# Linear attention into a soft mixture of experts: one DVE reduction moved ahead of another, a maximum taken a tile later, and input loads regrouped

## The chip, the cores and the metric

One core of a Trainium2 chip runs the kernel. The metric is device time in microseconds (us) of one execution, as the median of several runs; lower is better. Before the change it is 174.96 us (median of 3 runs, 174.92 to 174.98). All data is float32. Engines are named as in the profile: PE (matrix products), PEld (its weight loads), DVE, ACT and POOL (element by element work), SP (issues the transfers). Every transfer of this kernel is issued by SP on one queue, which 16 DMA engines serve.

## The reference

Eight batches of 576 tokens with eight heads of 64 go through linear attention; each head's output row is scaled by its root mean square; the 4608 rows of 512 then go through a soft mixture of eight experts with four slots each.

```python
kv = np.einsum('bhsd,bhse->bhde', k, v)
out = np.einsum('bhsd,bhde->bhse', q, kv)
rms = np.sqrt(np.mean(out * out, axis=-1, keepdims=True) + 1e-06)
x = (out / rms * g_norm)                      # rows: (batch, token), 512 columns
logits = x @ phi                              # 4608 x 32 slots
d = softmax of logits over the 4608 tokens
slot_input = d.T @ x                          # 32 x 512, four rows per expert
slot_out[e] = np.maximum(slot_input[e] @ w1[e], 0.0) @ w2[e]
c = softmax of logits over the 32 slots
result = c @ slot_out
```

## The kernel before

**Tiles.** The 4608 tokens are 36 tiles T of 128. For each tile PE multiplies q with a block diagonal tile `bd` of k times v of the batch (`products`, L273; L264 where a tile spans two batches) and gets in one go the attention output and its share of the logits per head, 192 columns for each pair of heads, in a PSUM tile `o` with two buffers. Two tiles make a stage s (the last two stages have one tile each). Of each tile ACT takes the squares (`square`, L283), the parts of the logits (`evict`, L290) and the rows x (L291). Of each stage DVE sums the squares (`mean_square`, L296, "ms"); ACT makes a reciprocal root from that (`root`, L304 and L305); DVE refines it (`newton`, L312 to L314, "r"); POOL scales the logits' parts (`scale_part`, L345) and then the rows (`scale_x`, L323); DVE adds the parts of the eight heads up to logits (`logits`, L358).

**Groups.** Six tiles make a group G. When its last logits are there, DVE takes a maximum over the group and all before it (`group_max`, L371 and L379), PE turns it (`group_max_T`, L386), DVE reduces it (`group_max_row`, L394), ACT and PE spread it (`group_diag`, L398; `group_exp_PE`, L403), DVE and ACT make exponentials (`group_exp`, L409, L410), and PE adds up exponentials times rows (`group_sum`, L422), which DVE gathers (L429). The dictionaries `T_at`, `diag_at`, `pb_at`, `d_at` and `sums_at` say at which tile each of these steps is emitted.

**Order.** Nothing is scheduled by a tool: each engine runs its instructions in the order in which the loop over T (L487) writes them. In one turn of it stand, for DVE, `logits` of the stage that ended two tiles ago, the group's maximum, `newton` of the stage that ended one tile ago, the group's reduced row, and `mean_square` of the stage that ends now. The products of k and v of the coming batch (`kv_step`, L205 to L250) are put between the tiles. Tiles 34 and 35 and the last group are written out behind the loop (L531 to L574).

**Experts.** `expert_h(e)` (L637) multiplies the slots with w1 of expert e; `expert_y(e, hf)` (L655) multiplies the result with w2 and adds all experts up, first the left half of the columns (hf = 0), then the right half (hf = 1). `output` (L688) multiplies with the combine weights; ACT and DVE copy the result (L696, L698) and SP sends it out in six transfers (L702). Matrices w2 of experts 2 to 7 are packed by halves: units 2, 3 and 4 hold the left halves of experts 2 and 3, 4 and 5, 6 and 7, and units 5, 6 and 7 the right halves. The left halves are multiplied in the order of the experts, so unit 3 is read before unit 4.

**Loads.** Nearly all of a core's fast memory is one tile `arena` of 128 partitions, in which q, k, v, weights and results follow each other in the same places. `KV_AT`, `Q_AT`, `W_AT` and `OUT_AT` give the places (in kilobytes of a partition), `W_ROWS` says which weights come in one transfer, one row of it for each of the 128 partitions. SP issues them in the order of the program (`load_head`, L90; `load_row`, L93; `load_w`, L122), each when what stood in its place has been read: `loads_behind` ties them to tiles, the rest stand behind the loop and between the experts. "t2" is batch 4's k and v with two batches of q, "kv5" is batch 5's k and v, "t3" batches 6 and 7 with their q.

Of the kernel before, what the change touches and what calls it, by code (L numbers as in the profile page):

```python
# [14 lines left out]
P = 128  # L15
# [15 lines left out]
TOK = 4608  # L31
# [4 lines left out]
KV_AT = (0, 36, 54, 0, 90, 126, 18, 54)  # L36
Q_AT = (18, 72, 108, 36)
W_AT = {
# [3 lines left out]
}  # L42
W_ROWS = (
    (("w1", 0, None), ("w2", 0, None)),
    (("w1", 1, None), ("w2", 1, None)),
    (("w1", 2, None), ("w1", 3, None)),
    (("w1", 4, None), ("w2", 2, 1)),
    (("w1", 5, None),),
    (("w1", 6, None),),
    (("w1", 7, None),),  # L50
    (("w2", 2, 0),),
    (("w2", 3, None),),
    (("w2", 4, None),),
    (("w2", 5, None),),
    (("w2", 6, None),),
    (("w2", 7, None),),
# [1 line left out]
OUT_AT = (16, 22, 28, 34, 40, 46, 72, 128, 134, 78, 84, 90)  # L58
OUT_ROWS = ((0, 1), (2, 3), (4, 5), (6,), (7, 8), (9, 10, 11))
HEAD = 144  # L60
SCRATCH = 1024
EPS_RMS = 1e-6
EPS_SUM = 1e-9
# [4 lines left out]


@with_exitstack  # L70
def soft_moe_linear_attention(ctx: ExitStack, tc: tile.TileContext, first_in, head_in, t2_in, kv5_in, t3_in, w_in, out):


    nc = tc.nc
# [17 lines left out]
    def load_row(at, src):  # L92
        nc.sync.dma_start(place(at, src.shape[-1]), src)  # L93
# [20 lines left out]
    def load_w(kind, u, part=None):  # L114
        i = [row[0] for row in W_ROWS].index((kind, u, part))
        lo = sum(row_length(row) for row in W_ROWS[:i])
        n = row_length(W_ROWS[i])
        src = w_in[:, lo * P : (lo + n) * P].rearrange("o (p n) -> (o p) n", p=P)
        t = homes(kind, u)[part or 0]
        if n > t.shape[-1]:  # L120
            t = place(W_AT[kind, u][part or 0], n)
        nc.sync.dma_start(t, src)  # L122

    def w_block(kind, u, i):
# [16 lines left out]
    loads_behind = {  # L141
        9: lambda: load_row(KV_AT[6], t3_in),
        18: lambda: load_w("w1", 0),
        21: lambda: load_w("w1", 1),
        26: lambda: load_w("w1", 2),
        27: lambda: load_w("w1", 4),
        31: lambda: load_w("w1", 5),
    }

    nc.scalar.preload_act_table_set("natural_log_exp_and_others")  # L150
# [134 lines left out]
    def evict(T, o):  # L285
        s = stage_of[T]
        if T == starts[s]:
            parts[s] = wk.tile([P, STAGES[s], H, NS], F32, tag="part", name=f"part{s}", bufs=3)
        part = parts[s][:, T - starts[s]].rearrange("p (j w) n -> p j w n", w=2)
        nc.scalar.copy(part, o[:, :, :192].rearrange("p j (c n) -> p j c n", n=NS)[:, :, 0::5])  # L290
        nc.scalar.copy(xts[T % NX][:, :, :128], o[:, :, 32:160])  # L291


    def mean_square(s):
        mss[s] = wk.tile([P, STAGES[s] * H], F32, tag="ms", name=f"ms{s}", bufs=3)
        nc.vector.tensor_reduce(  # L296
            out=mss[s], in_=sqs.pop(s).rearrange("p t j (w d) -> p (t j w) d", w=2), axis=AX.X, op=ALU.add
        )
# [84 lines left out]
    def group_max_T(G):  # L383
        pm = ps.tile([P, P], F32, tag="m", name=f"pm{G}")
        if G in tops:
            nc.tensor.matmul(pm, lhsT=tops.pop(G).rearrange("p a n -> p (a n)"), rhs=ident, start=True, stop=True)  # L386
        for j in range(4 if G == len(GROUPS) - 1 else 0):
            nc.tensor.matmul(
                pm[32 * j : 32 * j + 32], lhsT=L[:, pos(g0[G]) + GROUPS[G]], rhs=ident, start=True, stop=True
            )  # L390
        pms[G] = pm

    def group_max_row(G):
        nc.vector.tensor_reduce(out=run_max[G % 2], in_=pms.pop(G), axis=AX.X, op=ALU.max)  # L394
# [39 lines left out]
    first = {b: 9 * (b // 2) + 4 * (b % 2) for b in range(B)}  # L434
# [48 lines left out]
    load_head(4, 2048, TOK)  # L483
    load_row(KV_AT[4], t2_in)
    load_row(KV_AT[5], kv5_in)
    T_at, diag_at, pb_at, d_at, sums_at = {}, {}, {}, {}, {}
    for T in range(NT - 2):  # L487
        for b in range(1, B):
            for at in kv_steps.get((b, T - first[b]), ()):
                kv_step(b, at)  # L490
        o = products(T)
        s = ends.get(T - 1)
        if s is not None:
            root(s)
        if T in diag_at:
            group_diag(diag_at[T])
        square(T, o)
        G = d_at.get(T)
        if G is not None:
            group_exp(G)  # L500
            sums_at[T + 1] = G
        evict(T, o)
        old = ends.get(T - 2)
        if old is not None:
            logits(old)
            if (n := group_done(old)) is not None:
                group_max(n)
                T_at[T + 1] = n
        if T in T_at:
            group_max_T(T_at[T])  # L510
            diag_at[T + 1] = pb_at[T + 2] = T_at[T]
        if s is not None:
            newton(s)
        if T in T_at:
            group_max_row(T_at[T])
        if s is not None:
            scale_part(s, nc.gpsimd)
            scale_x(s)
        if T in pb_at:
            group_exp_PE(pb_at[T])  # L520
            d_at[T + 1] = pb_at[T]
        if T in ends:
            mean_square(ends[T])
        if T in sums_at:
            todo_sums += [(sums_at[T], i) for i in range(GROUPS[sums_at[T]])]
        for _ in range(min(2, len(todo_sums))):
            group_sum(*todo_sums.pop(0))
        if T in loads_behind:
            loads_behind[T]()
# [2 lines left out]
    tail_ps = ps.tile([P, 2, 512], F32, tag="kv", name="tail")  # L532
    A, Z = NT - 2, NT - 1
    oA = products(A)
    group_exp_PE(G - 1)
    root(s - 2)
    square(A, oA)
# [18 lines left out]
    group_max(G)  # L556
    for i in todo_sums:
        group_sum(*i)
    load_w("w1", 6)
    load_w("w1", 7)  # L560
    load_w("w2", 2, 0)
    fill(LATE_FILL[0], home=ps.tile([P, 512], F32, tag="m", name="fill"), cols=512)
    group_max_T(G)
    group_max_row(G)
# [139 lines left out]
                )  # L704

    expert_h(0)
    load_w("w2", 3)
    expert_h(1)
    load_w("w2", 4)
    expert_y(0, 0)  # L710
    combine(0)
    expert_h(2)
# [36 lines left out]
def build_program():  # L749
    import concourse.bacc as bacc  # L750

    nc = bacc.Bacc("TRN2", target_bir_lowering=False, num_devices=1, dynamic_dma_scratch_size=SCRATCH)
    shapes = {
        "first": (P, HEAD + 2304), "head": (6, P, TOK), "t2": (P, 2 * TOK), "kv5": (P, TOK), "t3": (P, 3 * TOK),
        "w": (1, 2 * NE * P * UNIT),
    }
    args = [nc.dram_tensor(f"in_{n}_dram", s, F32, kind="ExternalInput").ap() for n, s in shapes.items()]
    args.append(nc.dram_tensor("out_0_dram", (1, 4 * NCH * P * 4 * CT * NS), F32, kind="ExternalOutput").ap())
    with tile.TileContext(nc, schedule_with_timeline_sim=True) as tc, tc.manual_schedule():
        soft_moe_linear_attention(tc, *args)  # L760
    return nc
# [56 lines left out]
```

## Time and profile before

| What | Value |
|---|---|
| median of 3 runs | 174.96 us |
| the profiled execution | 174.76 us, of which its span (first to last instruction) is 173.0 us |
| outside the span | 1.76 us |
| PE busy | 150.3 us (87%) |
| DVE, ACT, POOL busy | 89.1 us, 86.4 us, 57.2 us |
| moved by DMA | 71.67 MB, 414 GB/s over the span |
| read from and written to HBM by the program | 61.94 MB and 9.44 MB |

The page gives an engine's busy time, its share of the span and its instructions; 40 equal slices of the span with the busy share in tenths; the DMA queues with packets, megabytes and the time of their packets as a share of 16 engines' span; the chain of work that ended last; and groups of instructions with busy time, the mean of one in nanoseconds, and the idle time of the engine just before them with what ended most of it. A view of DMA packets in a window counts the packets that start in it, by queue and size. In this program a row of a transfer is one packet, and each DMA engine closes a transfer with one packet of 4 bytes: the page counts 512 packets under 512 B, and 32 issues on 16 engines make 512. Queues that the page calls "instruction" bring in the program's own instructions.

### The profile page before, as it was taken

How to read it: one execution, taken by the hardware profiler on the slowest of the kernel's cores; microseconds unless marked ns; L12 is line 12 of the kernel's file. 1: busy time of each engine (PE TensorE's matmuls, PEld its weight loads, DVE VectorE, ACT ScalarE, POOL GpSimd, SP SyncE). 2: the span in 40 equal slices, each digit the busy share in tenths (PEclk: the TensorE clock that was granted, in tenths of full speed). 3: DMA queues.
4: the chain of work that ended last, by engine and by line, in shares of the span. 5: the costliest groups of instructions: out<-in, count | busy, mean ns of one | idle time of the engine just before them, and what ended most of it. 6: DMA issues, size and time to landing. Idle time of an engine off the chain costs nothing.

```text
span 173.0 us, 4659 instructions
## 1 busy us (share of the span) xinstructions
PE 150.3 (87%) x1973; PEld 108.3 (63%) x1973; DVE 89.1 (51%) x184; ACT 86.4 (50%) x224; POOL 57.2 (33%) x68
## 2 busy tenths in 40 slices
PE   7788999999979899999999796989999899978500
PEld 2467978888769788888897583346666435433200
DVE  1111456566576656566664776842888433456600
ACT  2024586976947976878859465112222131315500
POOL 6000067636557753477563676600000000000000
PEclk9999999999999999999999999999999999999955
DMA  5999999999999998999999999999999999999994
GB/s 199 420 429 427 447 404 447 399 506 409 405 413 473 479 435 359 417 436 415 440 440 415 426 411 421 424 432 415 434 419 424 424 424 425 393 404 418 418 452 196
DMA packets 4628, 71.67 MB, mean 414 GB/s; under 512 B 512, under 2 KB 512, under 8 KB 640
## 3 DMA queue, kind: packets, MB, share of 16 engines
q1 hardware_dynamic: 4608, 71.38, 97.3%
q8 instruction: 15, 0.25, 0.6%
q14 instruction: 5, 0.04, 0.1%
HBM read 61.94 MB, written 9.44 MB: 413 GB/s over the span
## 4 chain that ended last, share of the span: by engine, by line
PE 54%; DVE 16%; ACT 12%; POOL 5%; issue 4%; DMA 3%; POOLq 1%; DVEq 0%; ACTq 0%
PE o L273 13%; PE pY L655 9%; PE ph L637 8%; PE kvp_kv L205 7%; PE po L688 6%; POOL part L345 4%; DVE logits L358 4%; DVE ms L296 4%; DMA arena<-in_first_dram 3%; PE pS L422 2%; ACT sq L283 2%; DVE arena L698 2%; ACT bd L240 2%; ACT xall L291 1%; ACT r L304 1%
## 5 line engine op out<-in xcount | busy, mean ns | idle before, releaser
L273 PE MATMUL o<-bd,arena 128*128 128x192 f32 x256 | 49.3, 336 | 1.6 <-ACT xall L291 0.6
L273 PEld LDWEIGHTS o<-bd,arena 128*128 128x128 f32 x256 | 41.0, 191 | 4.4 <-ACT xall L291 1.7
L345 POOL TENSOR_TENSOR part<-part,r 128x512 f32<-128x512 f32 x17 | 17.8, 1047 | 52.6 <-DVE r L314 52.6
L323 POOL TENSOR_TENSOR xall<-xall,r 128x512 f32<-128x512 f32 x34 | 34.7, 1043 | 0.0
L358 DVE TENSOR_REDUCE logits<-part 128x64 f32<-128x512 f32 (+1 forms) x18 | 18.3, 1014 | 16.5 <-POOL part L345 16.4
L296 DVE TENSOR_REDUCE ms<-sq 128x16 f32<-128x1024 f32 (+1 forms) x19 | 21.9, 1154 | 5.8 <-ACT sq L283 5.7
L283 ACT ACTIVATE sq<-o 128x512 f32<-128x512 f32 x36 | 21.4, 596 | 6.1 <-PE o L273 5.8
L291 ACT COPY xall<-o 128x512 f32<-128x512 f32 x34 | 20.7, 609 | 0.0
L205 PE MATMUL kvp_kv<-arena 128*64 128x64 f32 x480 | 17.9, 231 | 0.9 <-DMA arena<-in_first_dram 0.9
L205 PEld LDWEIGHTS kvp_kv<-arena 128*64 128x64 f32 x480 | 15.9, 144 | 4.3 <-issue 1.9
L696 ACT COPY arena<-po 128x768 f32<-128x768 f32 x12 | 9.3, 800 | 18.5 <-PE po L688 18.4
L698 DVE COPY arena<-po 128x768 f32<-128x768 f32 x12 | 11.3, 956 | 10.6 <-PE po L688 9.8
L655 PE MATMUL pY<-arena,xall 128*32 128x256 f32 x256 | 15.6, 382 | 0.5 <-DVE y L671 0.5
L688 PE MATMUL po<-logits,z 32*128 32x384 f32 x96 | 13.5, 525 | 2.1 <-DVE z L677 0.9
L637 PE MATMUL ph<-arena,sTe 128*32 128x256 f32 x224 | 12.7, 380 | 0.3 <-DVE sTe L584 0.3
L655 PEld LDWEIGHTS pY<-arena,xall 128*32 128x32 f32 x256 | 7.8, 110 | 7.8 <-issue 1.4
L290 ACT COPY part<-o 128x256 f32<-128x256 f32 x34 | 12.6, 372 | 0.0
L304 ACT ACTIVATE r<-ms,eps 128x16 f32<-128x16 f32 x17 | 5.2, 308 | 14.7 <-DVE ms L296 14.5
L422 PE MATMUL pS<-xall,d 128*32 128x129 f32 x288 | 10.8, 278 | 2.0 <-ACT d L410 2.0
L688 PEld LDWEIGHTS po<-logits,z 32*128 32x128 f32 x96 | 5.8, 183 | 8.9 <-ACT arena L696 5.0
L637 PEld LDWEIGHTS ph<-arena,sTe 128*32 128x32 f32 x224 | 7.2, 110 | 5.3 <-DVE sTe L584 0.7
L422 PEld LDWEIGHTS pS<-xall,d 128*32 128x32 f32 x288 | 7.1, 109 | 5.1 <-issue 4.2
(93 smaller groups left out, 143.9 us busy)
## 6 DMA issues: line engine op xcount, KB each, us to landing
arena<-in_w_dram SPq DMA_DIRECT2D x7, 2048.0 KB, 17.6
arena<-in_w_dram SPq DMA_DIRECT2D x3, 4096.0 KB, 22.9
arena<-in_t_dram SPq DMA_DIRECT2D x1, 6912.0 KB, 36.1
out_dram<-arena SPq DMA_DIRECT2D x4, 1536.0 KB, 7.2
arena<-in_head_dram SPq DMA_DIRECT2D x2, 2304.0 KB, 22.5
arena<-in_t_dram SPq DMA_DIRECT2D x1, 4608.0 KB, 35.3
arena<-in_head_dram SPq DMA_DIRECT2D x3, 1152.0 KB, 11.9
arena<-in_w_dram SPq DMA_DIRECT2D x1, 3072.0 KB, 26.0
```

The costliest lines, as they stand in the source:

```text
L205: nc.tensor.matmul(self.pkv[lo : lo + 64, w, g], lhsT=main[:, w, 1, c, lo : lo + 64], rhs=main[:, w, 0, c, lo : lo + 64], start=c == 0 and ...
L273: nc.tensor.matmul(o[:, r, :192], lhsT=q_main(2 * g + i)[:, r, at : at + P], rhs=bds[i][:, r], start=True, stop=True)
L283: nc.scalar.activation(sqs[s][:, T - starts[s]], o[:, :, 32:160], AF.Square, scale=0.125)
L291: nc.scalar.copy(xts[T % NX][:, :, :128], o[:, :, 32:160])
L296: nc.vector.tensor_reduce(out=mss[s], in_=sqs.pop(s).rearrange("p t j (w d) -> p (t j w) d", w=2), axis=AX.X, op=ALU.add)
L323: nc.gpsimd.tensor_tensor(out=x, in0=x, in1=r[:, i].rearrange("p (j w) -> p j w", w=2).unsqueeze(3).to_broadcast([P, 4, 2, D]), op=ALU.mult,)
L345: engine.tensor_tensor(out=part, in0=part, in1=rs_of[s].unsqueeze(3).to_broadcast([P, STAGES[s], H, NS]), op=ALU.mult)
L358: nc.vector.tensor_reduce(out=L[:, pos(starts[s]) : pos(starts[s]) + STAGES[s]], in_=parts.pop(s).rearrange("p t h n -> p t n h"), axis=AX ...
L422: nc.tensor.matmul(pS[32 * j : 32 * j + 32], lhsT=ds[G][:, i], rhs=x[:, j], start=i == 0, stop=i == GROUPS[G] - 1)
L637: nc.tensor.matmul(ph[32 * j : 32 * j + 32], lhsT=sTe[:, (4 * e + c) * NS : (4 * e + c + 1) * NS], rhs=w_block("w1", e, 4 * c + j), start= ...
L655: nc.tensor.matmul(pY[32 * j : 32 * j + 32, hf, :256], lhsT=hTs[e][:, c], rhs=w_block("w2", u, at + c), start=e == 0 and c < 4, stop=e == ...
L688: nc.tensor.matmul(po[:, u, : CT * NS].rearrange("p (g x) -> p g x", g=2), lhsT=z[lo : lo + 32, f * P : (f + 1) * P], rhs=cT[k][lo : lo + 32],
```

## The change

1. **DVE's order.** `mean_square` of the stage that ends at tile T is emitted before `logits` of the stage that ended at T - 2, no longer at the end of the turn.
2. **The group's maximum.** Turning and reducing it (`group_max_T`, `group_max_row`) moves from one to two tiles behind the last logits' tile, to the head of the turn; the spread, the exponentials and the sums follow one tile later too. For group 4 the spread (`group_diag`) now stands behind the loop.
3. **Loads joined.** Units 3 and 4 of w2 come in one transfer of 8192 columns behind `expert_h(1)`, where unit 3 came behind `expert_h(0)` and unit 4 behind `expert_h(1)`. The left part of unit 2, w1 of expert 6 and w1 of expert 5 come in one transfer of 10240 columns behind the loop; before, w1 of expert 5 was issued at tile 31 and the other two behind the loop, one at a time. The first two pairs are sorted anew: w1 of experts 0 and 1 together, then w2 units 0 and 1.
4. **Batch 5.** Its transfer has 4352 of the 4608 columns. The last 256 columns (1 KB of each partition's row) come in three transfers of 44, 44 and 40 partitions from an input laid out in four shares: the outer dimension of the source has four entries of 11, 11 and 10 rows.

```diff
 W_AT = {
-    ("w1", 0): (72,), ("w2", 0): (88,), ("w1", 1): (128,), ("w2", 1): (144,), ("w1", 2): (0,),
+    ("w1", 0): (72,), ("w1", 1): (88,), ("w2", 0): (128,), ("w2", 1): (144,), ("w1", 2): (0,),
...
 W_ROWS = (
...
-    (("w2", 3, None),),
-    (("w2", 4, None),),
+    (("w2", 3, None), ("w2", 4, None)),
...
+APART_ROWS = ((0, 11), (11, 11), (22, 10))
...
-        21: lambda: load_w("w1", 1),
+        21: lambda: load_w("w2", 0),
         26: lambda: load_w("w1", 2),
         27: lambda: load_w("w1", 4),
-        31: lambda: load_w("w1", 5),
...
     load_row(KV_AT[5], kv5_in)
+    rest = place(KV_AT[5], TOK)[:, TOK - 256 :]
+    for at, n in APART_ROWS:
+        nc.sync.dma_start(rest[4 * at : 4 * (at + n)], rest_in[at : at + n].rearrange("p a n -> a p n"))
...
         evict(T, o)
+        if T in T_at:
+            group_max_T(T_at[T])
+            diag_at[T + 1] = pb_at[T + 2] = T_at[T]
+            group_max_row(T_at[T])
+        if T in ends:
+            mean_square(ends[T])
         old = ends.get(T - 2)
         if old is not None:
             logits(old)
             if (n := group_done(old)) is not None:
                 group_max(n)
-                T_at[T + 1] = n
-        if T in T_at:
-            group_max_T(T_at[T])
-            diag_at[T + 1] = pb_at[T + 2] = T_at[T]
+                T_at[T + 2] = n
         if s is not None:
             newton(s)
-        if T in T_at:
-            group_max_row(T_at[T])
-        if s is not None:
             scale_part(s, nc.gpsimd)
             scale_x(s)
         if T in pb_at:
             group_exp_PE(pb_at[T])
             d_at[T + 1] = pb_at[T]
-        if T in ends:
-            mean_square(ends[T])
...
     oA = products(A)
+    group_diag(G - 1)
     group_exp_PE(G - 1)
...
-    load_w("w1", 6)
+    load_w("w2", 2, 0)
     load_w("w1", 7)
-    load_w("w2", 2, 0)
...
     expert_h(0)
+    expert_h(1)
     load_w("w2", 3)
-    expert_h(1)
-    load_w("w2", 4)
```

More of the change, by code (lines that the diff above doesn't have):

```diff
@@ L38 @@
 W_AT = {
[1 row of a table removed]
[1 row of a table added]
     ("w1", 3): (16,), ("w1", 4): (104,), ("w1", 5): (56,), ("w1", 6): (40,), ("w1", 7): None,
[1 row of a table removed]
[1 row of a table added]
 }
 W_ROWS = (
-    (("w1", 0, None), ("w2", 0, None)),
-    (("w1", 1, None), ("w2", 1, None)),
+    (("w1", 0, None), ("w1", 1, None)),
+    (("w2", 0, None), ("w2", 1, None)),
     (("w1", 2, None), ("w1", 3, None)),
     (("w1", 4, None), ("w2", 2, 1)),
-    (("w1", 5, None),),
-    (("w1", 6, None),),
+    (("w2", 2, 0), ("w1", 6, None), ("w1", 5, None)),
     (("w1", 7, None),),
-    (("w2", 2, 0),),
-    (("w2", 3, None),),
-    (("w2", 4, None),),
+    (("w2", 3, None), ("w2", 4, None)),
     (("w2", 5, None),),
@@ L70, in soft_moe_linear_attention @@
 @with_exitstack
-def soft_moe_linear_attention(ctx: ExitStack, tc: tile.TileContext, first_in, head_in, t2_in, kv5_in, t3_in, w_in, out):
+def soft_moe_linear_attention(ctx: ExitStack, tc: tile.TileContext, first_in, head_in, t2_in, kv5_in, rest_in, t3_in, w_in, out):
     nc = tc.nc
@@ L753, in build_program @@
     shapes = {
-        "first": (P, HEAD + 2304), "head": (6, P, TOK), "t2": (P, 2 * TOK), "kv5": (P, TOK), "t3": (P, 3 * TOK),
+        "first": (P, HEAD + 2304), "head": (6, P, TOK), "t2": (P, 2 * TOK), "kv5": (P, TOK - 256), "rest": (P // 4, 4, 256), "t3": (P, 3 * TOK),
         "w": (1, 2 * NE * P * UNIT),
@@ L799 @@
     first[:, HEAD:] = kv[0, :, :2304]
+    rest = np.concatenate(
+        [kv[5][4 * at : 4 * (at + n), -256:].reshape(4, n, 256).transpose(1, 0, 2) for at, n in APART_ROWS]
+    )
     arrays = {
@@ L803 @@
         "in_t2_dram": np.concatenate([kv[4], qm[2]], axis=1),
-        "in_kv5_dram": kv[5],
+        "in_kv5_dram": np.ascontiguousarray(kv[5][:, :-256]),
+        "in_rest_dram": rest,
         "in_t3_dram": np.concatenate([kv[6], qm[3], kv[7]], axis=1),
```

2 rows, old and new, of the table W_AT are left out of this document.

## The prediction

> **What bounds the kernel now.** I read the page first, then windows of DMA packets, then SP's timeline beside PE's. From the page:
>
> ```profile
> span 173.0 us, 4659 instructions
> DMA  5999999999999998999999999999999999999994
> q1 hardware_dynamic: 4608, 71.38, 97.3%
> q8 instruction: 15, 0.25, 0.6%
> PE 54%; DVE 16%; ACT 12%; POOL 5%; issue 4%; DMA 3%; POOLq 1%; DVEq 0%; ACTq 0%
> ```
>
> The chain is made of PE, DVE and ACT, with 3% DMA, which reads like a compute-bound kernel. But the DMA engines are full from the second slice to the last but one: 97.3% of 173.0 us is 168.3 us of data for a mean engine. An engine with no pause cannot be helped by faster compute. So I asked whether all 16 engines are alike. The last load of weights (unit 7 of w2, first row below: its issue; second: 2048 KB, landed 21.4 us later, at 150.3) ends at each engine with a 4-byte packet; the windows 146.3 to 146.8, 146.8 to 148.6 and 149.4 to 150.0 count them ("under 512 B"), and the last two rows do so for the last output, in 170.3 to 170.6 and 171.5 to 171.9:
>
> ```profile
> 128.87 0.33 SPq L122 DMA_DIRECT2D arena<-in_w_dram  x1
> ...
> arena<-in_w_dram SPq DMA_DIRECT2D x1, 2048.0 KB, 21.4
> ...
> DMA packets 20, 0.23 MB, mean 451 GB/s; under 512 B 5, under 2 KB 5, under 8 KB 5
> DMA packets 58, 0.75 MB, mean 419 GB/s; under 512 B 5, under 2 KB 5, under 8 KB 5
> DMA packets 27, 0.26 MB, mean 437 GB/s; under 512 B 6, under 2 KB 6, under 8 KB 6
> ...
> DMA packets 13, 0.07 MB, mean 246 GB/s; under 512 B 9, under 2 KB 9, under 8 KB 9
> DMA packets 7, 0.00 MB, mean 0 GB/s; under 512 B 7, under 2 KB 7, under 8 KB 7
> ```
>
> Five engines end the same load about 3.2 us before six others. At the very end nine are through 1.2 us before seven. All carry the same bytes; what differs is the 15 instruction loads: 0.6% of 16 x 173.0 us is 16.6 us, 1.1 us each, and with the packets that they hold up a skew of 3.2 us is two of them on a late engine, none on an early one. Between the two places the early engines lost 2 us of their lead because they waited for SP:
>
> ```profile
> 154.70 0.33 SPq L702 DMA_DIRECT2D out_dram<-arena  x1
> ...
> 154.80:155.50 0.70, 0.40 (x4) 0.34 (x8) 0.16 (x1) 0.00 (x0) 0.00 (x0) 1.00 0.58 246
> ...
> 163.54 0.33 SPq L702 DMA_DIRECT2D out_dram<-arena  x1
> ...
> out_dram<-arena SPq DMA_DIRECT2D x1, 2304.0 KB, 8.6
> ```
>
> Just behind the third output's issue 0.58 of the engines work (seven or so idle); the other nine or so never stop. So the end, 163.54 + 8.6 = 172.1, is set by **seven late DMA engines that are full from the first transfer to the last**, with compute just ahead of them. The last transfer takes 8 rows of 18 KB, some 5.5 us, so the late engines, whose closing packets stand at about 171.7, begin it near 166.2; SP issued it at 163.54, and from issue to first packets an idle engine takes about 0.8 us (154.70 to 155.5). Compute has thus 166.2 - 164.4 = 1.8 us to spare against the late engines. That is the frame of the whole forecast.
>
> **Rows and bytes.** What a transfer costs an engine comes from two windows, 128 to 140 us (rows of 16 KB; 41 of its packets have 4 bytes) and 54.3 to 66.3 us (rows of 54 KB):
>
> ```profile
> DMA packets 354, 5.13 MB, mean 427 GB/s; under 512 B 41, under 2 KB 41, under 8 KB 41
> q1 hardware_dynamic: 352, 5.10, 100.0%
> ...
> q1 hardware_dynamic: 91, 5.03, 97.5%
> ```
>
> 16 x 12 us / (352 - 41) = 617 ns for 16384 B; 0.975 x 16 x 12 us / 91 = 2057 ns for 55296 B. The difference, 1440 ns for 38912 B, is 0.0370 ns a byte; that leaves 617 - 606 = 11 ns fixed for a row.
>
> **Part by part: the loads.** SP's order (t2, kv5, t3 and w name the inputs; 128x4608 is rows by columns) from batch 4 to the last weights, before:
>
> ```order
> L93 DMA arena_63<-in_t2_dram 128x9216
> L93 DMA arena_63<-in_kv5_dram 128x4608
> L93 DMA arena_63<-in_t3_dram 128x13824
> L122 DMA arena_63<-in_w_dram 128x8192 x3
> L122 DMA arena_63<-in_w_dram 128x6144
> L122 DMA arena_63<-in_w_dram 128x4096 x2
> L122 DMA xall_64<-in_w_dram 128x4096
> L122 DMA arena_63<-in_w_dram 128x2048
> L122 DMA arena_63<-in_w_dram 128x4096 x5
> ```
>
> Nine of these 13 weight transfers are single units or halves. The same stretch of SP with the change:
>
> ```order
> L91 DMA arena_63<-in_t2_dram 128x9216
> L91 DMA arena_63<-in_kv5_dram 128x4352
> L485 DMA arena_63<-in_rest_dram 44x1x256 x2
> L485 DMA arena_63<-in_rest_dram 40x1x256
> L91 DMA arena_63<-in_t3_dram 128x13824
> L120 DMA arena_63<-in_w_dram 128x8192 x3
> L120 DMA arena_63<-in_w_dram 128x6144
> L120 DMA arena_63<-in_w_dram 128x10240
> L120 DMA xall_64<-in_w_dram 128x4096
> L120 DMA arena_63<-in_w_dram 128x8192
> L120 DMA arena_63<-in_w_dram 128x4096 x3
> ```
>
> Three weight transfers are gone and three small ones are new. Joining: three rows fewer for each of an engine's 8 partitions, 3 x 8 x 11 ns = 0.26 us for every engine, late ones too. Batch 5: each engine moves 8 x 1024 x 0.0370 ns = 0.30 us less in the main transfer. Where its kilobytes go decides: a source whose outer dimension is four suggests four engines with 32 rows each: 32 x (38 + 11) ns = 1.57 us there, and nothing on the other twelve. If the four are early engines, they come to 1.57 - 0.30 = 1.27 us later than their lead of 3.2 us, still early, and the late ones gain 0.30. The trace shows no transfer of four shares, so this is bounded: a gain of 0.30 at best, a loss of 1.27 if the four hold a late one. I take the gain, since nine of 16 are not late (15 instruction loads with two on each of seven engines leave one for the nine).
>
> [...]
>
> Late engines: -0.26 - 0.30 = **-0.56 us**. On SP the three new issues stand between kv5 and t3:
>
> ```profile
> 14.03 0.33 SPq L93 DMA_DIRECT2D arena<-in_kv_dram  x1
> 34.59 0.33 SPq L93 DMA_DIRECT2D arena<-in_t_dram  x1
> ...
> arena<-in_kv_dram SPq DMA_DIRECT2D x1, 2304.0 KB, 40.2
> ```
>
> Three issues of 0.33 us are 1 us of the 20 us between the two, so they cost nothing; were t3 issued 10 us later for some wait of theirs, the queue would still be full, because kv5 lands at 54.2.
>
> **Joining delays unit 3.** It now lands with unit 4. Before, unit 4 was issued at 120.23 and landed 15.3 us later, at 135.5, just when PE asked for it:
>
> ```profile
> 120.23 0.33 SPq L122 DMA_DIRECT2D arena<-in_w_dram  x1
> ...
> arena<-in_w_dram SPq DMA_DIRECT2D x1, 2048.0 KB, 15.3
> ...
> 132.26 5.40 PE pY L655 x96
> ...
> 135.66 1.48 PEld L655 LDWEIGHTS pY<-arena,xall 128*32 128x32 f32 x32 [0.35 <-DVE xall L649]
> ```
>
> (The wait is put down to DVE; the landing at 135.53 is the nearer cause.) Now four of the six products (64 of 96 matmuls, 5.40 / 96 = 56 ns each) wait for 135.5 - 0.56 = 135.0: 135.1 + 3.6 = 138.7, against 132.26 + 5.40 = 137.7. So compute behind it runs **1.0 to 1.1 us later**, whatever the loop before it gains. That eats 1.1 of the 1.8 us to spare, and the late engines' 0.56 another part: 0.1 to 0.2 us is left. Taken alone it is free, just; without that cover each further 0.1 us would be 0.1 us at the end.
>
> **DVE's order.** Sums of squares (L296, now L293), logits (L358, now L355), refinement (L312 to L314, now L309 to L311) around the first group's end, before:
>
> ```order
> L314 SCALAR_TENSOR_TENSOR r2_348<-r12_349,r02_340 128x16
> L358 TENSOR_REDUCE logits_98<-part2_296 128x64
> L371 TENSOR_REDUCE logits_98<-logits_98 128x32
> L379 COPY top0_392<-logits_98 128x128
> L296 TENSOR_REDUCE ms3_394<-sq3_343 128x16
> L312 SCALAR_TENSOR_TENSOR r13_420<-ms3_394,r03_409 128x16
> ```
>
> The sum ms3 stands behind logits and the maximum. DVE at the same place with the change:
>
> ```order
> L311 SCALAR_TENSOR_TENSOR r2_351<-r12_352,r02_343 128x16
> L293 TENSOR_REDUCE ms3_393<-sq3_346 128x16
> L355 TENSOR_REDUCE logits_98<-part2_299 128x64
> L368 TENSOR_REDUCE logits_98<-logits_98 128x32
> L376 COPY top0_397<-logits_98 128x128
> L309 SCALAR_TENSOR_TENSOR r13_421<-ms3_393,r03_412 128x16
> ```
>
> ms3 no longer stands behind logits, which wait for POOL. What waited for it:
>
> ```profile
> ACT r L304 <- DVE ms L296: 14.5, 13, 2.5
> DVE logits L358 <- POOL part L345: 16.4, 16, 1.3
> PE pm L386 <- DVE top L379: 2.0, 3, 0.9
> ...
> 60.00:90.00 30.00, 30.00 (x455) 26.01 (x454) 18.54 (x39) 22.59 (x63) 16.40 (x18) 1.00 0.99 424
> 90.00:105.00 15.00, 12.75 (x118) 10.15 (x116) 9.62 (x20) 10.27 (x29) 8.07 (x8) 1.00 1.00 425
> ```
>
> Most of ACT's 14.5 us should go, and PE's 2.0 us with the later maximum. From 60 to 90 us PE is busy all 30.00, so only the rest can pay: 2.25 us of idle PE in 90 to 105, up to 2 us earlier. What is late next is PE itself. But at 135.0 compute waits for unit 3 anyway, so this is worth nothing at the end. It is needed in one place: the joined load of 10240 columns is issued when the loop's last products are done, 104.11 before, while the early engines run dry near 105 (window 104.9 to 105.2, three of 16 closing packets):
>
> ```profile
> 104.11 0.33 SPq L122 DMA_DIRECT2D arena<-in_w_dram  x1
> ...
> DMA packets 8, 0.10 MB, mean 328 GB/s; under 512 B 3, under 2 KB 3, under 8 KB 3
> ```
>
> 104.1 + 0.8 just meets it; late engines have 3 us more there. Group 4's spread behind the loop is one ACT operation and adds nothing to a chain that has 1.3 us to wait at unit 3.
>
> **The sum.** 174.76 (profiled) - 0.56 = 174.2; the median of the runs is 0.20 above the profiled execution: **174.4 us**.
>
> **Rivals.** *The kilobytes still cost the late engines.* Whichever engine carries a row, it goes to the same partition; if the receiving side sets the 27 GB/s of an engine (1 / 0.0370), an early engine's write holds up the late one whose partitions these are, and only the joining is left: 174.96 - 0.26 = 174.7. If the shares are spread over all 16, 8 x 11 ns come back: 174.8. For it: all row sizes give one rate, as a common limit would. Against it: nothing in the trace tells a limit of the sender from one of the receiver. [...] Chance 0.24.
>
> *The shares land on late engines.* Then those are the last by 1.27 - 0.26 = 1.0 us more: 176.0. It decides as soon as one of the four has two instruction loads. For it: nothing in the trace numbers the engines. Against it: nine of 16 are not late. Chance 0.11.
>
> *Compute becomes the bound.* If the tail behind unit 3 comes over 1.3 us later (say 2.5, by slower copies or a later landing), the last issue sets the end: 174.4 + 1.2 = 175.6; at 1.5 us, 174.6. Chance 0.11, half of it over 0.2%.
>
> *More is won.* If early and late engines also meet fewer instruction loads or less queueing, up to the whole 1.2 us of the last skew goes: 173.8. Chance 0.06.
>
> The forecast itself: 0.48.
>
> **Chances.** 0.2% of 174.96 is 0.35 us, about what a measurement of this kernel can tell from no change: faster is below 174.61. Forecast: 0.44 below, 0.04 within; more won: 0.06 below; the first rival within, 0.01 below; compute 0.05 within, 0.06 slower; shares on late engines 0.11 slower. Faster 0.51, same 0.32, slower 0.17. The range: 174.0 to 175.3 leaves out the 176.0 case, most of 173.8 and the worst of compute.
>
> **What would show it.** Right: the first loads' skew shrinks at unit 7's closing packets, the late ones near 149.7; of the closing packets 476 are left of 512 (29 transfers on 16 engines, three on four); PE waits about 1 us for DMA before the fourth of its products; the last output is issued near 164.6 and lands near 171.6; ACT's wait for ms falls below 5 us. Wrong: a landing at 173 with four engines last (shares on late engines), 512 closing packets as before (shares spread), late engines near 150.0 at unit 7 (receiving side), or all engines idle before the last output (compute).

## The result, and the profile after

The changed kernel takes **177.97 us** (median of 6 runs, 177.41 to 178.72) against 174.97 us before on the same chip (6 runs, 174.92 to 175.43): ratio 1.0167, 95% interval 1.0151 to 1.0182. It is slower by 3.0 us; the forecast was 0.6 us faster, range 174.0 to 175.3. The profiled execution took 177.80 us, 3.04 more than the one before.

From the page of the changed kernel: span, the row of the clock, DMA engines, packets, the main queue, the chain by engine and by line, and the group of the experts' second products:

```profile
span 176.0 us, 4649 instructions
PEclk9999999999999999999999999999999699999995
DMA  5999999999999998999999999999999998878996
DMA packets 4336, 71.67 MB, mean 407 GB/s; under 512 B 476, under 2 KB 604, under 8 KB 732
q1 hardware_dynamic: 4316, 71.38, 96.2%
PE 62%; DMA 13%; ACT 9%; DVE 6%; issue 3%; POOL 1%; POOLq 1%; DVEq 0%; ACTq 0%
...
L653 PE MATMUL pY<-arena,xall 128*32 128x256 f32 x256 | 17.3, 413 | 5.1 <-DMA arena<-in_w_dram 4.6
```

The bytes are the same, and the 476 closing packets are the forecast's count for three transfers on four engines each. But the DMA row, which before had nines in the last slices up to the very last, now has eights and a seven there; DMA's share of the chain went from 3% to 13%; one slice of the clock row shows 6; and in the last group PE waited 4.6 us for weights. The timeline of PE shows the place, first before, then after (start, length, instructions, idle time before them):

```profile
116.51 3.66 PE L637 MATMUL ph<-arena,sTe 128*32 128x256 f32 x64 [0.28 <-DVE sTe L584]
...
132.07 5.55 PE L655 MATMUL pY<-arena,xall 128*32 128x256 f32 x96
```

```profile
114.54 3.66 PE L635 MATMUL ph<-arena,sTe 128*32 128x256 f32 x64 [0.28 <-DVE sTe L582]
...
130.11 1.91 PE L653 MATMUL pY<-arena,xall 128*32 128x256 f32 x32
136.57 5.35 PE L653 MATMUL pY<-arena,xall 128*32 128x256 f32 x64 [4.56 <-DMA arena<-in_w_dram]
```

The loop gained its 2 us (experts start at 114.54, not 116.51) and PE spent them, and more, standing still for 4.56 us until the joined units 3 and 4 had landed. Then 64 matmuls took 5.35 us, 84 ns each, where 96 took 5.55, 58 ns each. Windows of the changed kernel around that stretch (the column behind POOL is the granted clock) say why:

```profile
132.00:136.50 4.50, 0.02 (x3) 0.00 (x0) 1.42 (x4) 0.47 (x1) 0.00 (x0) 1.00 0.95 404
136.50:137.50 1.00, 0.93 (x12) 0.65 (x16) 0.00 (x0) 0.00 (x0) 0.00 (x0) 0.59 0.96 410
137.50:138.50 1.00, 1.00 (x16) 0.62 (x11) 0.00 (x0) 0.00 (x0) 0.00 (x0) 0.50 1.04 442
138.50:139.50 1.00, 1.00 (x13) 0.60 (x9) 0.00 (x0) 0.00 (x0) 0.00 (x0) 0.50 1.00 426
139.50:140.50 1.00, 1.00 (x20) 0.73 (x16) 0.00 (x0) 0.00 (x0) 0.00 (x0) 0.71 1.00 426
```

After the standstill **the granted clock was halved**: the shortfalls 0.41 + 0.50 + 0.50 + 0.29 make 1.70 us lost, 3.4 us at half speed. The end follows. Last output of the changed kernel, the DMA packets from 173 us on, and windows of it (the column behind the clock is the share of the DMA engines' time):

```profile
167.84 0.33 SPq L700 DMA_DIRECT2D out_dram<-arena  x1
out_dram<-arena SPq DMA_DIRECT2D x1, 2304.0 KB, 7.3
...
DMA packets 48, 0.59 MB, mean 246 GB/s; under 512 B 16, under 2 KB 16, under 8 KB 16
...
154.40:155.20 0.80, 0.80 (x8) 0.26 (x12) 0.01 (x1) 0.49 (x1) 0.00 (x0) 1.00 0.00 0
159.20:159.80 0.60, 0.40 (x4) 0.34 (x8) 0.06 (x1) 0.00 (x0) 0.00 (x0) 1.00 0.00 0
160.00:169.00 9.00, 6.13 (x46) 2.54 (x39) 5.56 (x6) 4.70 (x6) 0.00 (x0) 1.00 1.00 415
```

It is issued at 167.84, 4.30 us later than before, and so is the third output (159.00 instead of 154.70). The last lands in 7.3 us, not 8.6, with all 16 engines through within about 0.2 us of each other: no engine is late any more, compute is the bound. The place where compute holds the engines up is not the last output, though: at 167.84 all 16 still move the rows of the fifth, until 169.2. It is ahead of the second and the third output, where all 16 stand idle (0.00 in the first two windows); from the third's first rows, at 159.8, they work without a pause to the end. Before the change the seven late engines ended the second output at about 157.0 and never stopped, though the third, issued at 154.70, could have had its first rows at 155.5. That is some 1.5 us of room; by the landings of the last output it is 8.6 - 7.3 = 1.3 us. The rest of the 4.30 us, 2.8 to 3.0, is the loss.

Three suspects follow: the joined landing with its standstill, the halved clock, and the shares of batch 5. The experiments separate them. (A ratio compares undisturbed runs only, so a median over all runs can lie above it.)

### The profile page after: what moved, and what is told of

Its sections match the earlier page's. It is cut to its first block, busy times and chain, and to the rows that moved or that the text cites. A ratio compares the mean times of both kernels' runs of the same rounds, so it can differ in the third digit from the quotient of the medians.

```text
span 176.0 us, 4649 instructions
## 1 busy us (share of the span) xinstructions
PE 153.0 (87%) x1973; PEld 110.9 (63%) x1973; DVE 87.2 (50%) x184; ACT 87.1 (49%) x224; POOL 57.2 (32%) x68
## 4 chain that ended last, share of the span: by engine, by line
PE 62%; DMA 13%; ACT 9%; DVE 6%; issue 3%; POOL 1%; POOLq 1%; DVEq 0%; ACTq 0%
PE o L270 23%; DMA arena<-in_w_dram 10%; PE kvp_kv L202 10%; PE pY L653 7%; PE po L686 6%; PE pS L419 3%; DMA arena<-in_first_dram 3%; PE o L261 3%; PE ph L635 2%; DVE arena L696 2%; PE kvp_kv L217 2%; ACT sq L280 2%; ACT xall L288 1%; ACT bd L237 1%; ACT arena L694 1%
## 5 line engine op out<-in xcount | busy, mean ns | idle before, releaser
L270 PE MATMUL o<-bd,arena 128*128 128x192 f32 x256 | 50.9, 343 | 1.4 <-ACT bd L247 1.1
L270 PEld LDWEIGHTS o<-bd,arena 128*128 128x128 f32 x256 | 42.3, 196 | 4.7 <-ACT bd L247 1.6
L653 PE MATMUL pY<-arena,xall 128*32 128x256 f32 x256 | 17.3, 413 | 5.1 <-DMA arena<-in_w_dram 4.6
L653 PEld LDWEIGHTS pY<-arena,xall 128*32 128x32 f32 x256 | 9.0, 118 | 12.9 <-issue 8.1
L462 PE MATMUL fill<-zeros 128*128 128x512 bf16 x26 | 8.3, 476 | 1.1 <-DVE zeros L154 1.1
```

Of the source, the lines that this page charges most:

```text
L270: nc.tensor.matmul(o[:, r, :192], lhsT=q_main(2 * g + i)[:, r, at : at + P], rhs=bds[i][:, r], start=True, stop=True)
L653: nc.tensor.matmul(pY[32 * j : 32 * j + 32, hf, :256], lhsT=hTs[e][:, c], rhs=w_block("w2", u, at + c), start=e == 0 and c < 4, stop=e == ...
```

## The experiments

**Undoing one part each.** Units 3 and 4 in two transfers again, the rest of the change kept:

```diff
-    (("w2", 3, None), ("w2", 4, None)),
+    (("w2", 3, None),),
+    (("w2", 4, None),),
```

> Units 3 and 4 of w2 in two transfers again, all else as changed. Theory A (the joined load lets PE stand still for 4.56 us, the granted clock then halves, and compute issues the last output too late): PE waits only for unit 4, some 3 us with half the products left; the left half's products end near 138.3 to 139.6 and not at 141.9; the late DMA engines, 0.8 to 0.9 us behind those of before since the small transfers, then set the end: 175.4 to 176.0 us. Theory B (the small transfers alone, by slowing the other rows at 52 to 57 us, set the end): about as changed, 177.5 or more. Theory C (DVE's order or the later maximum costs time): about as changed.

Median 176.84 us (8 runs), ratio 1.009 (1.0065 to 1.0115). The profiled execution was the fastest, 175.62, in the expected range; three runs lay at 175.6 to 175.8 and five at 176.8 to 177.2. Of 3.0 us the join holds 0.9 or 2.2, by the medians of the two groups.

Batch 5 in one transfer again (`kv5` of 4608 columns, no `rest`), the rest kept:

> Batch 5 in one transfer again, all else as changed. Theory A: units 3 and 4 land near 135.3, PE still waits 3.5 us or so and the clock still halves, the left half's products end near 140.7, the last output is issued near 166.6: 176.5 to 177.0 us. Theory B: the loss is gone, 174.6 to 175.0 us. Theory C: about as changed, 177.5 or more.

177.33 us (4 runs), ratio 1.0129 (1.0099 to 1.0159), above the 176.5 to 177.0 expected. PE still waits 4.43 us, and the 64 matmuls behind that take 5.94 us instead of 5.35: here the clock was halved from 133.42, still within the wait, to 140.24. The shares are not the main loss.

Both undone, which leaves the loop's order and the join of 10240 columns:

> Both undone: units 3 and 4 apart and batch 5 whole; what is left of the change is DVE's order, the later maximum, and the join of the left part of unit 2 with w1 of experts 6 and 5. Theories A and B: no loss, 174.6 to 175.0 us, since the late DMA engines set the end and the join saves them 0.13 to 0.17 us. Theory C: 176 us or more.

175.25 us (10 runs), ratio 1.0017 (0.9999 to 1.0035): as before, though above the 174.6 to 175.0 expected. Its last output is issued at 164.92, just inside the room: ahead of the third output about seven engines never stop. PE waits there 2.11 us for unit 4, and the clock halves after it as well; that it costs nothing at the end is due to the room alone.

**The clock.** Twenty idle products in the wait, in the changed kernel:

```diff
     for e in range(NE - LATE, NE):
+        if e == 4:
+            fill(20, home=ps.tile([P, 2, 512], F32, tag="m", name="warm")[:, 1], cols=512)
         expert_y(e, 0)
```

> The changed kernel with 20 idle products (the kernel's own fill, into a spare PSUM tile) in front of the fourth expert's left half, so that PE works on while it waits for units 3 and 4. Theory A: granted clock 1.00 instead of 0.5 from 136.5 to 140, the 64 matmuls behind the wait take 3.6 us instead of 5.35, the end comes about 1.7 us earlier, 175.9 to 176.4 us. If the wait alone and not the clock made the loss, or the end is set by DMA alone (B): 177.4 to 178.

178.44 us (4 runs), ratio 1.0191 (1.0151 to 1.0231): the total missed. Its timeline of PE, then its last issue, an instruction load in a window at 164 us, and the time to landing:

```profile
130.85 4.49 PE L462 MATMUL warm<-zeros 128*128 128x512 bf16 x20
136.08 3.66 PE L653 MATMUL pY<-arena,xall 128*32 128x256 f32 x64 [0.74 <-DMA arena<-in_w_dram]
...
165.67 0.33 SPq L700 DMA_DIRECT2D out_dram<-arena  x1
...
q8 instruction: 1, 0.02, 27.4%
...
out_dram<-arena SPq DMA_DIRECT2D x1, 2304.0 KB, 9.2
```

The step held: the same 64 matmuls in 3.66 us instead of 5.35, the last output issued 2.17 us sooner. The experiment then spoiled its own end: with its 40 added instructions (4689, not 4649) came a sixteenth instruction load at 164.0, and one DMA engine closed the last output at 174.4, 1.8 us behind the other 15. That this engine is the one that carried the load is argued from the times, and the other three runs were not profiled.

So the next fills the wait with work that adds no instruction: the right halves of experts 0 and 1, in place for long.

```diff
     for e in range(NE - LATE, NE):
+        if e == 4:
+            expert_y(0, 1)
+            expert_y(1, 1)
         expert_y(e, 0)
...
-    expert_y(0, 1, range(4))
...
-    expert_y(0, 1, range(4, 8))
...
-    expert_y(1, 1)
```

> The changed kernel with the right halves of experts 0 and 1, whose weights have long been in place, computed ahead of the left half of expert 4, so in the time in which TensorE waits for the joined units 3 and 4; no instruction more, none less, no load moved. (A) The loss is mostly compute behind the joined landing (a standstill of 4.56 us, then products at half the clock): the wait falls by the 1.75 us of the two moved experts to about 2.8 us, and the last output is issued 1.75 us earlier than the 167.84 us of the changed kernel, at about 166.1 us, which gives about 176.1 us; if so short a standstill leaves the granted clock whole, 1.75 us more come off the compute, the last issue is near 164.3 us, and the DMA engines set the end, later than before by what the shares of batch 5 cost them: 175.4 to 175.9 us. (B) The DMA engines alone made the loss: 177.4 to 178.0 us, with the last output issued earlier and its landing as late as in the changed kernel.

176.13 us (10 runs), ratio 1.0048 (1.0029 to 1.0067): theory A. The wait is 3.52 us and not 2.8, because PE reached it almost 1 us sooner in this execution (132.8, where 132.0 + 1.75 was due); the clock still halves (64 matmuls in 5.35 us), and the last output goes at 166.22. Three of the ten runs took 175.2 to 175.4, as they would with a whole clock; their mean granted clock over the span, 0.966, cannot tell, since the other seven have 0.951 to 0.972.

Then three long idle products behind these, six records of matmuls in all:

```diff
             expert_y(1, 1)
+            warm = ps.tile([P, 2, 512], F32, tag="m", name="warm")[:, 1]
+            for i in range(3):
+                nc.tensor.matmul(warm, lhsT=sel.rearrange("p a n -> p (a n)"), rhs=homes("w2", 1)[0][:, :512], start=True, stop=True)
         expert_y(e, 0)
```

> The changed kernel with the right halves of experts 0 and 1 and three idle full-array products of 128x512 f32 ahead of the left half of expert 4. The idle products compute nothing that is used; by the 0.70 us of a 128x256 f32 full-array product they last some 2.5 us, so that TensorE stands still for about 1 us instead of 3.5 us. (A) The clock halves because TensorE stands still, and costs some 1.7 us: the clock stays whole, the last output is issued near 164.5 us (166.2 us with the right halves alone), and the DMA engines set the end: 175.2 to 175.5 us in nearly all runs, as in the faster three of the ten runs with the right halves alone. What is left above the kernel before, 0.2 to 0.5 us, is the shares of batch 5 on the DMA engines, less what the joined rows give. (B) The clock is lowered by something else, or the groups of runs have nothing to do with it: runs at 176.1 us as often as before (seven of ten).

175.41 us (9 runs, eight of them 175.23 to 175.65), ratio 1.0023 (0.9999 to 1.0046): theory A. Timeline of PE and SP's last issue:

```profile
129.28 3.64 PE L653 MATMUL pY<-arena,xall 128*32 128x256 f32 x64
132.85 2.84 PE L726 MATMUL warm<-arena,sel 128*128 128x512 f32 x6
136.34 3.66 PE L653 MATMUL pY<-arena,xall 128*32 128x256 f32 x64 [0.65 <-DMA arena<-in_w_dram]
...
164.55 0.33 SPq L700 DMA_DIRECT2D out_dram<-arena  x1
out_dram<-arena SPq DMA_DIRECT2D x1, 2304.0 KB, 8.2
```

The landing is as late as ever (136.34), the clock stays whole, and the last output goes at 164.55, 3.29 us sooner than in the changed kernel: 1.62 by the halves moved into the wait (167.84 to 166.22), 1.67 by the clock. That takes away 2.56 of the 3.0 us with no load changed.

The same with batch 5 in one transfer:

> The same with batch 5 in one transfer: all joins and the new order of the loop, right halves and idle products in the standstill. (A) Compute no longer sets the end, and no shares delay the DMA engines: 174.7 to 174.95 us, the kernel before less at most the 0.26 us of the joined rows. (B) The joined rows give nothing even with all that out of the way: 174.95 to 175.2 us, same as before.

174.97 us (11 runs), ratio 1.0001 (0.9984 to 1.0019), beside 174.99 for the kernel before: nearer to B. So the shares cost 175.41 - 174.97 = 0.44 us where nothing else is in the way, and the joins give nothing that can be seen.

**The same wait, with and without the halved clock.** One more profile of the version with units 3 and 4 apart:

> The changed kernel with units 3 and 4 apart, once more for one profile: eight runs of it fell into two groups (175.6 to 175.8 and 176.8 to 177.2 us), of which only the lower has been seen in a profile, with the clock whole. (A) The groups are the clock: a profiled run of the upper group shows slices at half the clock behind the wait for unit 4 and a last output issued about 1.7 us later than 164.3 us; one of the lower group shows none. (B) An upper run with a whole clock.

This execution took 176.12 us. First the execution of 175.62 us, then this one (PE, SP):

```profile
136.48 1.94 PE L654 MATMUL pY<-arena,xall 128*32 128x256 f32 x32 [2.95 <-DMA arena<-in_w_dram]
...
164.34 0.33 SPq L701 DMA_DIRECT2D out_dram<-arena  x1
```

```profile
136.54 3.20 PE L654 MATMUL pY<-arena,xall 128*32 128x256 f32 x32 [2.97 <-DMA arena<-in_w_dram]
...
165.72 0.33 SPq L701 DMA_DIRECT2D out_dram<-arena  x1
```

One kernel, waits of 2.95 and 2.97 us, and the clock halves in one execution only: 1.38 us later at the last issue, 0.5 us in the time. So the length of the wait alone does not decide it: 2.11 us halved the clock above, and 2.95 us did not here. The runs of 176.8 to 177.2 us have not been seen in a profile. The halved clock behind this wait gave 176.12; their mean granted clocks, 0.950 to 0.960 against 0.965 to 0.972 in the lower group, point to more time at half speed, but where is open.

The traces say more about the chance. Within each profile the changes of the clock lie whole multiples of 3.413 us apart, as marks of a fixed beat (in the changed kernel it is halved at 136.68, whole at 140.09 and lowered at 170.81: 3.413 us and nine times that), and the halved stretch begins not with the standstill but at a mark (136.68 in the changed kernel, 137.05 in the execution above, 136.14 in the version with both parts undone). So what counts, as far as these traces tell, is how much PE worked between two marks. Three stretches from mark to mark (PE's busy time is the second number): ahead of the halving in the execution of 176.12 us and in the version with both undone, then behind the mark that cut the wait of the 175.62 us execution in two:

```profile
133.63:137.05 3.42, 0.51 (x12) 0.42 (x16) 0.00 (x0) 0.00 (x0) 0.00 (x0) 1.00 1.01 431
```

```profile
132.73:136.14 3.41, 1.30 (x24) 0.60 (x20) 0.47 (x2) 0.00 (x0) 0.00 (x0) 1.00 0.99 423
```

```profile
134.61:138.02 3.41, 1.54 (x29) 1.13 (x32) 0.00 (x0) 0.00 (x0) 0.00 (x0) 1.00 0.99 423
```

At these products the clock was halved behind the stretches with 0.51 and 1.30 us of work, as in the changed kernel behind the one with 0.11 (133.26 to 136.68), and stayed whole behind the one with 1.54. The waits of 2.95 and 2.97 us thus differ in where a mark falls in them. This is read from traces, not tested by an experiment, and these amounts hold for these products alone: near the end of the kernel before, where other products run, the clock was lowered at 164.00 behind a stretch with 1.85 us of work (160.59 to 164.00).

**The loop and the joins, each alone.** The kernel before with nothing but the new order of DVE and of the maximum:

> The kernel before with the new order of the loop and nothing else: every load as before. (A) The loop ends 2 us sooner, and TensorE reaches the products of unit 4 that much sooner, so the gain turns into a wait of about 2 us for unit 4, which lands no earlier; whether the clock halves after it or not, the last output is issued before 165.3 us, up to where the compute has room, and the DMA engines set the end: 174.9 to 175.3 us. (B) The faster loop asks for weights sooner and collides with transfers: 175.5 us or more, with closing packets of loads later than before. (C) It gains at the end too: 174.0 to 174.5 us.

175.16 us (10 runs), ratio 1.001 (0.9991 to 1.0029): theory A. The experts start at 113.50, 3.0 us sooner than before, and PE waits 2.94 us for unit 4. All of the gain became waiting.

All joins, batch 5 in one transfer, and the loop in its old order:

> All three joins of the change with the loop in its old order and batch 5 in one transfer. (A) The joined landing of units 3 and 4 near 135.4 us sets when four of the six late products can start, whatever the loop does; the wait is shorter than the 4.43 us that the same loads gave with the new order, by the loop's 2 us: about 2.4 us. If the clock halves after it, the last output is issued near 167.4 us and the time is 177.0 to 177.4 us; if it stays whole, near 165.7 us and 175.4 to 175.9 us. (B) The new order of the loop is what costs time, by the length of the standstill or in any other way, and the join is free as the prediction had it: 174.7 to 175.1 us.

176.52 us (10 runs, 175.37 to 178.6), ratio 1.0053 (1.0026 to 1.008). In the profiled execution (176.10 us), PE and SP:

```profile
135.77 3.66 PE L651 MATMUL pY<-arena,xall 128*32 128x256 f32 x64 [1.37 <-DMA arena<-in_w_dram]
...
165.35 0.33 SPq L698 DMA_DIRECT2D out_dram<-arena  x1
```

Its wait is a second shorter than expected, with the clock whole, and the time is 0.2 above A's range for a whole clock. Rival B, that the join is free without the faster loop, falls: the last output is 1.8 us later than before. With the new loop the same loads gave 177.33. One more profile of it, because four of the ten runs lay at 178.2 to 178.6:

> All joins with the old order of the loop, once more for one profile: its ten runs fell into 175.4 to 176.6 us and 178.2 to 178.6 us, and the profiled one, of 176.1 us, had a wait of 1.37 us and the clock whole. (A) A run of the upper group shows half the clock behind the wait and a last output issued some 1.7 us or more later than 165.35 us. (B) An upper run with a whole clock, whose delay lies elsewhere, in a landing.

175.86 us, a wait of 1.16 us, the clock whole: a run of the lower group again. What the four runs met stays open.

Last the best guess at a faster kernel: the new loop and the join of 10240 columns, units 3 and 4 apart, batch 5 whole, right halves moved ahead of expert 6:

> The order of the loop and the join of three loads alone (units 3 and 4 apart, batch 5 in one transfer), with the right halves of experts 0 and 1 ahead of the left half of expert 6, where that version stood still for 2.11 us. (A) The wait falls by 1.75 us to 0.3 to 0.5 us, the granted clock stays whole, the last output is issued near 162 to 163 us, and the seven late DMA engines set the end as before: 174.7 to 174.9 us, that is before less the 0.14 to 0.26 us of the joined rows. (B) Something else in the new order of the loop costs time: 175.2 us or more, with the wait gone all the same.

175.03 us (12 runs), ratio 1.0016 (0.9993 to 1.0039), between the two ranges. The wait is 1.22 us, not 0.3 to 0.5, the clock whole, the last output issued at 163.16 and landed 9.1 us later: the late DMA engines are the bound again, and nothing is won. No version beat the kernel before.

**What a transfer on four engines costs.** Four kernels add 128 KB of useless loads to the kernel before, just ahead of t3. First the shape of the change, 1 KB rows in three transfers of 44, 44 and 40 partitions:

```diff
+    spare = place(144, 4096)
+    for at, n in ((0, 11), (11, 11), (22, 10)):
+        nc.sync.dma_start(
+            spare[4 * at : 4 * (at + n), :256], kv5_in[4 * at : 4 * (at + n), :256].rearrange("(p a) n -> a p n", a=4)
+        )
```

> The kernel before with 128 KB more to load (the first 256 columns of batch 5 once again, into a spare place behind batch 5's load), as three transfers of 44, 44 and 40 partitions from a source with an outer dimension of four, 1 KB a row: what the change adds, alone. Theory A (such transfers slow the rows of all other engines): rows of the next load (54 KB) that start from 52 to 57 us take 2.4 to 2.7 us instead of 2.05, and the late engines come about 1.1 us later, 176.0 to 176.4 us. Theory B (they only cost the four engines that carry them, which are early): 174.9 to 175.2 us.

The same bytes as one ordinary transfer of 128 partitions (`place(144, 256)`):

> The same 128 KB more in one ordinary transfer of 128 rows of 1 KB over all 16 engines. If small rows slow everything: rows of the next load slow, 176 us. If it is only work: 8 x (38 + 11) ns = 0.4 us on every engine, 175.3 to 175.5 us.

The same bytes in 4 KB rows on four engines, into partitions 0 to 15 and 32 to 47 (`spare[at : at + 16, :1024]`, at 0 and 32), or into partitions 64 to 95 (`spare[64:96, :1024]`):

> The same 128 KB more in rows of 4 KB on four engines, in two transfers to partitions 0 to 15 and 32 to 47. If small rows are what slows the others: no slow rows, 174.9 to 175.2 us. [...] If any four-engine transfer does it: as with rows of 1 KB, 176 us.

> The same 128 KB more in rows of 4 KB on four engines, in one transfer to partitions 64 to 95. If small rows are what slows the others: no slow rows, 174.9 to 175.2 us. If writing into other engines' partitions does: rows that start from 52 to 57 us are slow, and the end is 0.3 to 1.1 us later, 175.4 to 176.2 us.

In that order: 176.04 us, ratio 1.005 (1.0019 to 1.0081); 175.52, 1.0026 (1.0008 to 1.0044); 175.35, 1.0014 (0.9994 to 1.0034); 176.35, 1.0073 (1.005 to 1.0096). The first lies in A's range; the others lie 0.02, 0.15 and 0.15 us above the ranges that fit their rows. DMA packets from 52 to 57 us, where the small transfers and t3's first rows run: before, after, and the four in that order:

```profile
DMA packets 70, 2.57 MB, mean 514 GB/s; under 512 B 16, under 2 KB 16, under 8 KB 16
```

```profile
DMA packets 191, 1.95 MB, mean 389 GB/s; under 512 B 24, under 2 KB 152, under 8 KB 152
```

```profile
DMA packets 197, 2.02 MB, mean 404 GB/s; under 512 B 28, under 2 KB 156, under 8 KB 156
```

```profile
DMA packets 212, 2.59 MB, mean 518 GB/s; under 512 B 32, under 2 KB 160, under 8 KB 160
```

```profile
DMA packets 106, 2.48 MB, mean 496 GB/s; under 512 B 24, under 2 KB 24, under 8 KB 56
```

```profile
DMA packets 90, 1.85 MB, mean 371 GB/s; under 512 B 20, under 2 KB 20, under 8 KB 52
```

(A packet counts where it starts, so these rates compare kernels and are none of the engines.) The closing packets above the 16 of before, in the four 12, 16, 8 and 4, make four engines of each added transfer but the ordinary one. What slows the stretch is not small rows: 1 KB rows spread over 16 engines leave 518 GB/s, with 46 ns for a row by the trace's packet records. Nor is it the use of four engines: in x2 a 4 KB row takes 159 ns, and t3's rows of 54 KB their usual 2.04 us. But the same rows into partitions 64 to 95 take 259 ns in the mean, and t3's rows on other engines up to 3.2 us. The change's shares belong to this kind: their rows take 65 ns against the ordinary transfer's 46, and t3's rows that start in this stretch take 2.37 us in the mean (before 2.06; in the four kernels 2.36, 2.06, 2.06 and 2.51). Which partitions the four engines write is what the slow kernel and the harmless one differ in, besides one transfer instead of two; the number of transfers alone does not order them, since the first has three and is slow. Why rows on other engines slow down too is not shown.

## Why the prediction was wrong

- **"Joining delays unit 3 … free, just"** is the step that failed. It priced the delay at 1.0 to 1.1 us; it was 4.30. By PE's rows the left halves end at 136.57 + 5.35 = 141.92 instead of 132.07 + 5.55 = 137.62. Of that 4.3: the landing is 136.57, where 135.0 was forecast and unit 4 alone came at 135.53 (1.04; part of that is the shares, since joined landings ended PE's waits at 136.1 to 136.6 with them and at 135.6 to 136.1 without); behind the landing stand four products, 3.66 us at the full clock, instead of the two that the wait for unit 4 governed (2.09 left at that landing): 1.57; and the halved clock is 1.69. In the step's own terms (135.1 + 3.6 = 138.7, measured 141.92): 1.5 us too little for the landing, and nothing for the clock. Why the joined landing is late even without the shares is open.
- **The clock** was in no term and no rival. It is the part that experiments show most directly: 5.35 us against 3.66 us for the same 64 matmuls as the standstill goes from 3.52 to 0.65 us.
- **"Worth nothing at the end"** was right for the loop's gain alone (ratio 1.001), but the step took the wait as harmless. With the joins and batch 5 whole the new loop costs more than the old: 177.33 us and a halved clock in the one profile, against 176.52 us and a whole clock in both.
- **"1.8 us to spare"** was too much by 0.3 to 0.5, and read at the wrong place. At the last output the engines still have the fifth to move; the room ends ahead of the third, where the late engines have 157.0 - 155.5 = 1.5 us (1.3 by the landings).
- **The kilobytes of batch 5**, forecast at -0.30 us on the late engines, cost +0.44. The rival that placed the limit at the receiving side was nearer, but its worst was no gain. The four engines and the 476 packets were right.
- **The joined rows**, -0.26 us, did not show: 1.0001, with an interval down to 0.9984, which 0.26 us (0.9985) just touches. Unit 7 lands at 150.27 before and at 150.33 with all joins, batch 5 whole and the wait filled, where -0.26 was due. Whether the 11 ns a row are not saved by longer rows or were lost in gaps is open.
- **Right**: ACT's wait for ms fell (14.5 to 5.1 us, where below 5 was named), the loop ended 2 us sooner, and the shares did not cost the 1.0 us that a late engine carrying them would have (no trace numbers the engines). Engines idle before an output were named as the sign that compute had become the bound, though they stood idle before the second and the third, not the last. That rival had 0.11 and 2.5 us; it came with 4.3.

## What to carry to other kernels

Two loads that are read one after the other should not be joined where the first is read just as it lands: the join moves all work behind the first to the later landing. A wait on PE is priced with what the clock does behind it; here a standstill of 2.97 us already cost 1.38 us more at the last issue than one of 2.95 us, by where it fell in the clock's beat, and work moved into it gained on both accounts: 1.62 us by two experts' right halves, 1.67 us by the clock with three idle products behind them. And a gain that ends in a wait should be carried forward to that wait's consequences before it is called free.

## What the runs showed of the hardware

- Standstills of PE ahead of these products, with the clock behind them: halved after 4.56, 4.43, 3.52, 2.97 and 2.11 us; whole after 2.95, 2.94, 1.37, 1.22, 1.16, 0.74, 0.65 and 0.32 us. From 2.11 to 2.97 us either happened. Of the stretches of 3.413 us from mark to mark that were read there, those with 0.11, 0.51 and 1.30 us of work had the halved clock behind them, the one with 1.54 us the whole.
- A transfer on four engines into partitions 64 to 95 slowed rows of others from 2.06 to 2.51 us in the mean and to as much as 3.2 us; two transfers of the same bytes into partitions 0 to 15 and 32 to 47 slowed none.
- Instructions are load too: twenty idle products came with a sixteenth instruction load of 0.88 us on the DMA engines, and one of the 16 ended 1.8 us late.
